# Five matmul groups and two DMA issues change places in a hand-written order

## The chip, the cores and the metric

The kernel runs on one core of a Trainium2 chip. The metric is the device time of one execution in microseconds (us); lower is better. A core has five engines that run their own instruction streams and meet through semaphores: TensorE (PE, matrix products into PSUM; its weight loads are shown apart as PEld), VectorE (DVE), ScalarE (ACT), GpSimd (POOL) and SyncE (SP, which here only issues DMAs). PSUM, where products land, has eight banks of 128 x 512 floats.

## What is computed

Two branches share one layer norm of q (2048 rows of 512), and their results are joined:

```python
xn = _layernorm(x)                                  # x = A_q
# branch A: a long convolution per channel, done in the reference with FFTs
k_shift = sum(k_pad[:, t:t + S, :] * shift_k[:, ks - 1 - t] for t in range(4))
kv = k_shift * v
y = causal_conv(kv, ssm_k) + kv * ssm_D             # over 2048 positions
s = xn * y
# branch B: a gated feed-forward layer, 512 -> 1792 -> 512
g = silu((gelu(xn @ w_gate) * (xn @ w_up)) @ w_down)
out = x + s * g
```

(The convolution and the sum over taps are abridged here.)

## The kernel before

**Branch A** is a Fourier transform in two stages, done as matrix products. Stage 1 multiplies by a table `F1`: for the filter (called H and J; its transposed halves are `HTr` and `HTD`) in `half1` (line 919) and `stage1_h` (line 929), for kv in `stage1_k` (line 956). kv is made in place in `V`, so the profile shows these last products as `psall<-V,F`; they are called V's products here, and there are two of them, each of two 512-column matmuls, for every index u from 0 to 7. A stage 1 product goes to a PSUM bank pair, is copied by ACT or DVE into a staging buffer (`AST`, `ASX`, or parts of `X` and `G` that are not in use yet), and is stored by DMA to `ZH` (filter) or `ZK` (kv) in device memory. Stage 2 loads blocks `BH` and `BK` from there in another order, multiplies in 32 x 32 tiles (line 1028), multiplies the two spectra and goes back.

**Branch B** works in four blocks q of 512 rows: transposes of the normalized rows (`xn_transpose`, line 841), 14 units of a gate and an up product (`unit`, line 1109), and the down products of four row tiles (`down`, line 1143), which are cut into three pieces of 4, 5 and 5 matmuls. All ordinary matmuls go through the helper at line 618, so the profile shows them with that line.

**The order is written out by hand.** Every piece of work is a numbered task; the string `SEQ` lists all tasks, and `Sched.run` (line 345) walks it. Each engine executes its tasks in the order in which they stand in `SEQ`; between engines only data and buffers order the work. While it walks, a planner with estimated durations also picks buffers: a pool (`Pool_.find`, line 250) gives the free slot that has been free the longest by the planner's estimate. PSUM banks come from three pools over the same eight banks: `psF` (one bank, at most four in use), `psC` (a pair of banks) and `psX` (one bank, for transposes). A slot is given back where the last task that reads it stands in `SEQ`, so a task's place in the list also decides which bank it can get. Semaphore waits are derived from the buffers, so every order that the planner can fill with slots is correct.

Three details matter around the change:

- The staging buffers of J are `X[12:14]`, `X[14:16]` and two parts of `G`; those of kv are three (`AST` 0, `AST` 1, `ASX`). The load of the fourth row block of q, `X3` (task 48, line 772), overwrites `X[12:16]` and so waits until every store to `ZH` has landed (line 981).
- SP issues its DMAs strictly in order: one that waits holds up all behind it.
- V's product u=6, part 0 (task 255) is copied out by task 256 into `AST` 0, which held u=2 before; 256 therefore waits until the store of u=2 (task 239) has landed. Task 262, a later product of V, needs the bank pair that 256 empties.

Tasks that are named below:

| task | engine | work |
|---|---|---|
| 84, 85 | PE | transposes of row tiles 2 and 3 of block 0 (four small matmuls each) |
| 109, 110 | PE, ACT | filter product `HTr` u=5, second half (two 256-column matmuls); its copy to staging |
| 370, 378 | PE | up products of block 0, units 0 and 1, first halves (four 256-column matmuls each) |
| 434, 438, 448 | PE | pieces of down products of block 0: 434 has five matmuls, 438 and 448 four each |
| 242, 243, 244 | PE, ACT, SP | V's product u=3, part 1; its copy; the store of u=3 to `ZK` |
| 250, 251 | PE, ACT | V's product u=5, part 0; its copy to `ASX`, which held u=3 |
| 137, 138, 139 | PE, ACT, SP | filter product J5; its copy; its store to `ZH` |
| 122, 123, 124 | PE, ACT, SP | filter product J0; its copy; its store to `ZH`, the last one |
| 48, 239 | SP | load of X3; store of u=2 to `ZK` |
| 526, 491 | PE | gate product of block 1, unit 13; up product of block 1, unit 4 (four 512-column matmuls each) |
| 257, 262 | PE | V's products u=6 part 1 and u=7 part 1 |
| 640, 646, 647 | DVE | layer-norm statistics of two tiles of X3 and an aggregation |
| 451, 452 | ACT, DVE | the gate function on the down product of task 448, which empties its bank |

The profile's names: `psall` is PSUM, `Wu`, `Wg` and `Wd` are the up, gate and down weights, `HT` is the hidden layer.

Of the kernel before, what the change touches and what calls it, by code (L numbers as in the profile page):

```python
# [25 lines left out]
ORDER = "x02 h0 h1 x22 w0 w1 h2 h3 D0 w2 s0 k0 v0 x1 w3 k1 v1 d0 d1 k2 v2 k3 v3 x2 x3"  # L26
SEQ = (
    "17 18 0 3 1 2 4 8 5 7 11 20 6 9 50 12 65 66 67 73 19 68 75 74 49 10 76 13 52 21 82 22 86 117 83 69 107 70 71 112 54 72 87 77 78 53 369 51 "
    "108 36 56b 79 84 371 109 88 80 370 15 85 372 23 31 89 110 378 377 113 27 373 379 381 383 375 14 453 455 457 380 24 458 374 459 25 454 118 "
    "382 119 55 456 460 32 120 376 389 102 384 397 399 28 30 33 461 34 29 37 63 38 111 385 387 393 16 59 463 386 103 462 388 464 391 398 104 26 "  # L30
    "400 390 395 105 465 146 394 405 396 99 147 121 466 148 468 150 407 57 409 100 401 403 46 392 402 406 149 151 470 35 404 152 39 96 413 408 "
    "469 410 472 153 467 411 101 415 473 412 421 154 414 416 58 471 155 422 417 61 423 424 106 429 156 97 114 158 93 60 62 431 44 425 426 427 428 "
    "115 418 498 159 43 419 98 420 41 94 90 160 502 500 91 499 95 474 475 92 501 476 161 157 518 504 503 430 81 477 225 432 478 520 227 479 116 "
    "162 226 480 505 163 40 228 506 134 519 166 164 521 42 167 481 140 183 45 508 229 135 168 514 141 143 136 144 515 128 486 516 517 129 230 488 "
    "490 169 232 507 47 231 131 165 170 492 125 142 443 233 433 126 132 509 171 482 240 444 445 137 184 241 234 235 174 172 127 138 64 236 175 "
    "434 242 133 145 438 446 243 173 122 439 182 123 245 484 176 177 246 440 130 178 247 435 447 179 248 180 139 237 238 181 250 244 448 441 436 "
    "437 124 249 48 483 449 252 251 450 253 485 260 239 451 261 640 255 646 647 452 510 512 185 442 511 256 513 257 642 491 258 262 526 644 643 "
    "190 263 487 254 186 493 641 527 645 259 264 195 648 489 528 187 522 494 188 189 495 529 649 496 523 652 524 651 191 192 650 716 540 525 535 "
    "497 550 556 552 196 536 557 553 193 197 265 537 198 538 266 554 267 270b 278 268 555 291 541 542 279 280 530 200 531 653 269 194 532 304 283 "
    "551 558 271 199 272 292 533 562 561 543 296 559 560 545 546 547 293b 534 544 273 539 682 654 274 276b 684 655 275 656 277 281 201 548 282 "  # L40
    "563 674 657 202 284 285 683 685 203 658 660 205 662 675 549 294 664 286 676 295 289 287 297 298 663 204 659 661 317 670 299 677 592 302 600 "
    "594 300b 301 305 665 306b 593 330 672 307 309 602 671 673 206 308 207 595 712 208 210 568 612 614 570 209 613 310 596 318 319 601 615 322b "
# [1244 lines left out]
```

## Time and profile before

| what | value |
|---|---|
| time, median of 3 runs | 196.22 us (195.83 to 196.37) |
| the profiled execution's own time | 195.05 us |
| its span, first to last instruction | 193.3 us |
| PE busy | 186.7 us, 97% |
| DVE, ACT busy | 159.8 us (83%), 125.0 us (65%) |
| DMA | 49.19 MB, mean 255 GB/s |

The profile is one execution. Its own time is 1.75 us above its span, for what lies around the instructions, and 1.17 us below the median of the runs. A matmul's record lasts longer than the engine needs before the next one can start, since matmuls are pipelined: rows of one kind show one start every 0.216 us for 512 columns, so time that PE loses is read between starts, and the "idle before" in brackets understates it. A few matmul records are missing (30 of the 32 of `psall<-V,F` are there).

### The profile page before, as it was taken

The page shows a single profiled execution, that of the slowest core. Times are in us where ns is not written, and L with a number is a line of the kernel's source. Part 1 is how long each engine was busy: PE and PEld are TensorE (multiplying, and loading weights), DVE is VectorE, ACT ScalarE, POOL GpSimd, SP SyncE. Part 2 cuts the span into 40 slices and gives each one's busy share as a digit, 9 for nine tenths or more (in the row PEclk, how much of TensorE's full clock was granted, in tenths as well). Part 3 has the DMA queues.
Part 4 walks back from the last instruction along what each step waited for, and adds up shares of the span by engine and source line. Part 5 has one row for each costly group of instructions (what it writes and reads, how often), then busy time and mean ns, then how long its engine had stood idle before and what let it go on. Part 6 is the DMA issues. An engine that isn't in the chain of part 4 may idle for free.

```text
span 193.3 us, 3491 instructions
## 1 busy us (share of the span) xinstructions
PE 186.7 (97%) x1364; PEld 84.7 (44%) x1377; DVE 159.8 (83%) x245; ACT 125.0 (65%) x170; POOL 13.9 (7%) x32
## 2 busy tenths in 40 slices
PE   7799999999999999999999999999999999999993
PEld 2674544444444344343434433433444334444442
DVE  6799879998999993977888789878897863588993
ACT  6788899969866987868548766856577431232121
POOL 5512600000000000020300000000000000000000
DMA  5999999899999868999999981892705344939433
GB/s 181 326 300 360 380 405 331 182 254 378 335 381 337 243 221 262 356 333 317 256 308 221 345 270 58 292 333 86 262 13 196 105 140 136 407 114 325 158 139 136
DMA packets 45958, 49.19 MB, mean 255 GB/s; under 512 B 12787, under 2 KB 39671, under 8 KB 45942
## 3 DMA queue, kind: packets, MB, share of 16 engines
q1 hardware_dynamic: 37366, 42.67, 69.5%
q10 hardware_dynamic: 8576, 6.29, 10.3%
q8 instruction: 11, 0.18, 0.4%
q14 instruction: 5, 0.04, 0.1%
HBM read 27.39 MB, written 14.68 MB: 218 GB/s over the span
## 4 chain that ended last, share of the span: by engine, by line
PE 80%; DMA 10%; ACT 3%; DVE 2%; issue 1%; POOL 1%; SPq 0%; ACTq 0%
PE psall L618 74%; DMA ZH<-X 5%; PE psall L1028 5%; DMA ZK<-AST 3%; DMA X<-in_A_q_dram 2%; ACT X L609 2%; POOL mv L832 1%; ACT AST L609 1%; DVE stats L821 1%; PE psall L854 1%; DVE XN L835 0%; ACT G L1164 0%; POOL mv L831 0%; DVE HTr L612 0%; DVE G L1175 0%
## 5 line engine op out<-in xcount | busy, mean ns | idle before, releaser
L618 PE MATMUL psall<-xnT,Wu 128*128 128x512 bf16 (+1 forms) x232 | 55.8, 372 | 0.0
L618 PE MATMUL psall<-xnT,Wg 128*128 128x512 bf16 (+1 forms) x232 | 55.3, 372 | 0.0
L618 PE MATMUL psall<-Wd,HT 128*128 128x512 bf16 (+2 forms) x231 | 50.8, 366 | 0.7 <-issue 0.5
L1140 DVE TENSOR_TENSOR HT<-psall,GE 128x512 bf16<-128x512 f32 x54 | 36.6, 685 | 15.3 <-PE psall L618 14.1
L1137 ACT ACTIVATE GE<-psall 128x512 bf16<-128x512 f32 x54 | 31.6, 600 | 13.7 <-PE psall L618 13.0
L618 PEld LDWEIGHTS psall<-Wd,HT 128*128 128x128 bf16 x238 | 22.4, 98 | 25.8 <-issue 1.1
L618 PEld LDWEIGHTS psall<-xnT,Wg 128*128 128x128 bf16 x232 | 22.0, 98 | 25.2 <-issue 1.3
L618 PEld LDWEIGHTS psall<-xnT,Wu 128*128 128x128 bf16 x232 | 21.6, 98 | 25.9 <-issue 3.5
L609 ACT ACTIVATE X<-psall 128x1024 bf16<-128x1024 f32 (+1 forms) x18 | 15.0, 842 | 3.9 <-DMA ZH<-X 3.7
L609 ACT ACTIVATE HS<-psall 128x1024 bf16<-128x1024 f32 x14 | 13.7, 1022 | 4.1 <-PE psall L1028 4.1
L1164 ACT ACTIVATE G<-psall 128x512 bf16<-128x512 f32 x12 | 7.0, 597 | 12.6 <-PE psall L618 12.4
L1011 DVE TENSOR_TENSOR KAC<-KAC,KTM 128x2048 bf16<-128x2048 bf16 x12 | 14.6, 1217 | 0.1
L1009 DVE TENSOR_TENSOR KTM<-KK,SKB 128x2048 bf16<-128x2048 bf16 x12 | 14.6, 1217 | 0.0
L609 ACT ACTIVATE BO<-psall 128x1024 bf16<-128x1024 f32 x9 | 9.1, 1023 | 8.2 <-PE psall L1028 7.7
L821 DVE BATCH_NORM_STATS2 stats<-X 128x6 f32<-128x512 bf16 x16 | 10.3, 676 | 3.8 <-DMA X<-in_A_q_dram 3.8
L609 ACT ACTIVATE KB<-psall 128x1024 bf16<-128x1024 f32 x11 | 11.0, 1021 | 3.6 <-PE psall L1028 3.6
L609 ACT ACTIVATE AST<-psall 128x1024 bf16<-128x1024 f32 x12 | 12.3, 1034 | 1.5 <-PE psall L618 0.9
L612 DVE CAST BO<-psall 128x1024 bf16<-128x1024 f32 x7 | 8.5, 1223 | 3.7 <-PE psall L1028 3.7
L1172 ACT ACTIVATE G<-psall 128x512 bf16<-128x512 f32 (+2 forms) x5 | 2.6, 512 | 13.1 <-PE psall L618 13.1
L1091 DVE TENSOR_TENSOR HW<-KB,HW 128x1024 bf16<-128x1024 bf16 x16 | 10.9, 682 | 0.0
L1091 DVE TENSOR_TENSOR HS<-KB,HS 128x1024 bf16<-128x1024 bf16 x16 | 10.8, 682 | 0.0
L618 PE MATMUL psall<-V,F 128*128 128x512 bf16 x30 | 8.8, 380 | 0.5 <-ACT AST L609 0.3
(83 smaller groups left out, 171.2 us busy)
## 6 DMA issues: line engine op xcount, KB each, us to landing
BH<-ZH SPq DMA_DIRECT2D x8, 512.0 KB, 5.8
HW<-HS SPq DMA_DIRECT2D x16, 256.0 KB, 3.3
BK<-ZK SPq DMA_DIRECT2D x8, 512.0 KB, 5.2
ZI<-BO ACTq DMA_DIRECT2D x16, 256.0 KB, 3.0
BI<-ZI SPq DMA_DIRECT2D x8, 512.0 KB, 4.5
ZK<-AST SPq DMA_DIRECT2D x6, 512.0 KB, 4.5
Hn<-in_A_ssm_k_dram SPq DMA_DIRECT2D x4, 512.0 KB, 8.0
KK<-in_A_k_dram SPq DMA_DIRECT2D x4, 512.0 KB, 8.9
```

The source lines that it names most:

```text
L609: return h.activation(o, i, ACTF.Copy, scale=scale)
L612: return h.tensor_copy(o, i)
L618: return h.matmul(o, lhsT=l, rhs=r, start=st, stop=sp)
L821: t_stats[t] = op([("DVE", 670.0)], lambda e, h, t=t: h.bn_stats(stats[:, t, :], X[:, t, :]), r=[bX[q][t % 4]], w=[bst[t]], rr=[R_X[t]], w ...
L1009: op([("DVE", dur)], lambda e, h, j=j, m=m: h.tensor_tensor(KTM[:, m.slot, :, :], kk(j), sk(j), ALU.mult), r=need + [bSKB[j], a], w=[m], r ...
L1011: op([("DVE", dur)], lambda e, h, m=m: h.tensor_tensor(KAC[:, a.slot, :, :], KAC[:, a.slot, :, :], KTM[:, m.slot, :, :], ALU.add), r=[m], ...
L1028: trk.op("PE", lambda h: h.matmul(ps(s, i)[b, :], lhsT=wt(col)[a, :], rhs=data(col)[a, :], start=n < 16, stop=n >= len(todo) - 16, tile_po ...
L1091: return hd.tensor_tensor(o, flat(KB, kb[h]), o, ALU.mult)
L1137: op([("ACT", act(512))], lambda e, h: h.activation(GE[:, g.slot, :], bank(pg), ACTF.Gelu_apprx_tanh), r=[pg], w=[g], rr=lambda: R_bank(pg ...
L1140: op([("DVE", dve(512, 1))], lambda e, h: h.tensor_tensor(HT[:, q % 2, m, :], bank(pu), GE[:, g.slot, :], ALU.mult), r=[pu, g], w=[bHT[q][m]],
L1164: op([("ACT", act(n))], lambda e, h, g=g, pc=pc: h.activation(g, pc(), ACTF.Tanh, scale=0.5), r=[p], w=[bt], rr=lambda p=p: R_bank(p), ww= ...
L1172: op([("ACT", act(n))], lambda e, h, g=g, pc=pc: h.activation(g, pc(), ACTF.Silu), r=[p], w=[bt], rr=lambda p=p: R_bank(p), ww=rg, after=z ...
```

## The change

Only the string `SEQ` differs:

```diff
-    "108 36 56b 79 84 371 109 88 80 370 15 85 372 ...
+    "108 36 56b 79 84 371 88 80 370 15 85 109 372 ...
...
-    "434 242 133 145 438 446 243 ... 246 440 130 178 247 435 447 179 248 180 139 237 238 181 250 244 448 441 436 "
-    "437 124 249 48 483 449 252 251 450 253 485 260 239 451 261 640 255 646 647 452 510 512 185 442 511 256 513 257 642 491 258 262 526 644 643 "
+    "434 438 242 133 145 446 243 ... 246 440 130 178 244 247 435 447 179 248 180 139 237 238 181 448 441 250 436 "
+    "437 124 249 483 449 252 251 450 253 485 260 451 261 48 640 239 255 452 510 646 512 185 442 511 256 513 257 642 258 647 526 262 644 643 491 "
...
-    "497 550 556 552 196 536 557 553 193 197 265 ...
+    "497 550 556 552 557 553 193 196 197 536 265 ...
```

Sorted by engine, this is what moves against work of the same engine:

| engine | before | after |
|---|---|---|
| PE | 84, 109, 370, 85, 378 | 84, 370, 85, 109, 378 |
| PE | 434, 242, 438, 122 | 434, 438, 242, 122 |
| PE | 237, 250, 448, 483 | 237, 448, 250, 483 |
| PE | 257, 491, 262, 526, 487 | 257, 526, 262, 491, 487 |
| DVE | 640, 646, 647, 452, 442, 513, 642, 644 | 640, 452, 646, 442, 513, 642, 647, 644 |
| SP | 130, 139, 244, 124, 249, 48, 239 | 130, 244, 139, 124, 249, 48, 239 |

The order on ACT, on POOL and in the list of loads stays as it is. The other moved numbers (48, 239, 451, 510, 512, 196, 536 and so on) pass only tasks of other engines; they change where slots are taken and given back. Nothing is added or removed: the same instructions run.

6 rows, old and new, of the table SEQ are left out of this document.

## The prediction

> **What bounds the kernel now.** I read the page first, then the waits of PE, then its timeline around each wait, then the chain, and last the DMA queue behind the wait that matters most.
>
> ```profile
> span 193.3 us, 3491 instructions
> PE 186.7 (97%) x1364; PEld 84.7 (44%) x1377; DVE 159.8 (83%) x245; ACT 125.0 (65%) x170; POOL 13.9 (7%) x32
> ```
>
> PE is busy from end to end. An edit can only win time in which PE waits, and a new wait costs its full length. Two of PE's waits, in the view of waits (a third stands in the timeline below):
>
> ```profile
> PE psall L618 <- ACT AST L609: 0.3, 1, 0.3
> PE psall L618 <- ACT X L609: 0.2, 1, 0.2
> ```
>
> PE's timeline around all three (start, length, work, in brackets the idle time):
>
> ```profile
> 9.94 0.40 PE L854 MATMUL psall<-ident,XN 128*128 128x128 bf16 x4
> 10.54 0.39 PE L618 MATMUL psall<-HTr,F 128*128 128x256 bf16 x2 [0.20 <-DVE HTr L612]
> 10.77 0.60 PE L618 MATMUL psall<-xnT,Wu 128*128 128x256 bf16 x4
> 11.21 0.39 PE L854 MATMUL psall<-ident,XN 128*128 128x128 bf16 x4
> 11.43 0.60 PE L618 MATMUL psall<-xnT,Wu 128*128 128x256 bf16 x4
> ...
> 59.05 0.61 PE L618 MATMUL psall<-V,F 128*128 128x512 bf16 x2
> 59.49 2.32 PE L618 MATMUL psall<-Wd,HT 128*128 128x512 bf16 x10
> 61.65 0.59 PE L618 MATMUL psall<-HTD,F 128*128 128x512 bf16 x2
> ...
> 62.51 1.24 PE L618 MATMUL psall<-Wd,HT 128*128 128x512 bf16 x5
> 63.92 0.60 PE L618 MATMUL psall<-V,F 128*128 128x512 bf16 x2 [0.17 <-ACT X L609]
> ...
> 77.96 1.03 PE L618 MATMUL psall<-xnT,Wu 128*128 128x512 bf16 x4
> 79.28 0.38 PE L618 MATMUL psall<-V,F 128*128 128x512 bf16 x1 [0.28 <-ACT AST L609]
> ```
>
> Ten matmuls from 59.49 to 61.65 give one start every 0.216 us; the four transposes from 11.21 give 0.055 each, the four short matmuls from 10.77 give 0.11. The time lost between starts is then: before 109, 10.54 - (9.94 + 0.22) = 0.38; before 242, 63.92 - (62.51 + 5 x 0.216) = 0.33. At 262 the record of the first of two matmuls is missing, so it began at 79.28 - 0.216 = 79.06; PE was free at 77.96 + 4 x 0.216 = 78.82. Lost: 0.24.
>
> The chain from 45 to 85 us says what the late ones hang on:
>
> ```profile
> 51.20 6.68 DMA ZH<-X
> ...
> 57.96 1.03 ACT X L609
> ...
> 59.01 3.81 DMA ZH<-X
> ...
> 62.84 1.03 ACT X L609
> ...
> 72.03 5.91 DMA ZK<-AST
> ...
> 77.97 1.03 ACT AST L609
> ```
>
> Each is a copy by ACT that waits until a store has left its staging buffer: a store to ZH for the product at 59.05 and for 242 (released at 62.84 + 1.03 = 63.87), and for 262 the store of u=2, task 239, landed at 72.03 + 5.91 = 77.94.
>
> **The change, part by part.**
>
> *109 behind 370 and 85.* DVE's timeline at this place:
>
> ```profile
> 9.80 0.68 DVE L612 COPY HTr<-psall 128x1024 bf16<-128x1024 bf16 x1
> 10.40 0.41 DVE L835 TENSOR_SCALAR XN<-X,mv 128x512 bf16<-128x512 bf16 x1
> ```
>
> DVE's copy ends at 10.48 and 109 started at 10.54, so a hop costs 0.06. In the new order 370 starts at 10.16 and ends at 10.60. 85 needs the rows that DVE ends at 10.81 and now waits itself, to 10.87; it ends at 11.09, 109 at 11.31. 378 started at 11.43, so PE is 0.12 ahead: a third of the wait, the rest has moved to 85. The three tasks exchange banks; following the planner's pick by hand, bank pairs are only renamed afterwards, and I find no new owner that would wait. PE does not keep the 0.12: at 59.05 it meets a copy whose store was 6.68 us in a full queue, and nothing here makes that queue shorter. I count 0; the ends are -0.12 and 0.
>
> *438 ahead of 242.* Four down matmuls fill the wait from 63.59, and 242 starts at 63.59 + 0.864 = 64.45, after its release. The 0.33 is gone. Behind it stands ACT:
>
> ```profile
> 63.76 1.02 ACT L609 ACTIVATE AST<-psall 128x1024 bf16<-128x1024 f32 x1
> 65.15 1.04 ACT L609 ACTIVATE ASX<-psall 128x1024 bf16<-128x1024 f32 x1
> 66.05 1.05 ACT L609 ACTIVATE X<-psall 128x1024 bf16<-128x1024 f32 x1
> ```
>
> Copy 243 (65.15) gets its product at 64.45 + 0.60 (the length of the pair at 63.92) = 65.05, still before ACT is free: covered by 0.1. 122, next on PE at 64.88, needs the pair that the first row empties at 64.78, with the hop 64.84: covered by 0.04; without that cover 122 is late by as much. PE runs 0.33 ahead from here to 262.
>
> *448 ahead of 250.* PE is dense here, so nothing is won. The copy of 250 stands on ACT behind two gate functions, which hide the 0.86 by which 250 comes later; without them its store would be late by up to 0.86, with nobody waiting before the second stage. 0.
>
> *526 in the place of 491, 452 earlier on DVE.* One group of four stands ahead of 262 before and after, so its wait gets no cover. But 526 needs the bank that 452 empties, and 452 stands behind 640, which waits for X3:
>
> ```profile
> 76.69 1.29 DVE L821 BATCH_NORM_STATS2 stats<-X 128x6 f32<-128x512 bf16 x2 [2.98 <-DMA X<-in_A_q_dram]
> 78.11 1.25 DVE L1166 SCALAR_TENSOR_TENSOR G<-G,psall 128x512 bf16<-128x512 bf16 x2
> ```
>
> Half of 1.29 each: 452 starts at 77.34, takes 0.63 to 0.7, and 526 can start near 78.05, ending at 78.91. PE would be there at 77.96 - 0.33 = 77.63. So most of the wait moves from 262 to 526; it ends ahead of the release of 262 at 79.06 with 0.15 to spare, and if X3 is later, both are later together. 491 and 647, which come later, have readers on DVE that are further behind. 0; beyond the cover it would cost what is over 0.15.
>
> *244 ahead of 139 on SP.* SP's timeline and its longest wait for a DMA, then the DMA queues from 66 to 74 us, first the rate in 40 slices of 0.2 us, and from the page the row of instruction fetches:
>
> ```profile
> 63.89 0.50 SPq L590 DMA_DIRECT2D ZH<-X  x1
> 66.21 0.33 SPq L590 DMA_DIRECT2D ZK<-ASX  x1
> 67.13 0.36 SPq L590 DMA_DIRECT2D ZH<-X  x1
> 71.64 0.34 SPq L590 DMA_DIRECT2D X<-in_A_q_dram  x1
> 72.03 0.43 SPq L590 DMA_DIRECT2D ZK<-AST  x1
> ```
>
> ```profile
> SPq L590 <- DMA ZH<-X: 1.3, 1, 1.3
> ```
>
> ```profile
> GB/s 277 67 0 0 0 307 451 451 389 287 328 341 236 274 292 282 172 23 20 20 41 20 15 164 392 389 392 471 389 389 82 20 0 143 184 184 205 164 164 61
> q8 instruction: 1, 0.02, 1.1%
> ZK<-ASX SPq DMA_DIRECT2D x1, 512.0 KB, 4.7
> ZH<-X SPq DMA_DIRECT2D x1, 256.0 KB, 4.5
> ```
>
> ```profile
> q8 instruction: 11, 0.18, 0.4%
> ```
>
> 139, issued at 63.89 so far, now stands behind 244, which waits for copy 243 until 66.21; so 139 goes out at 66.54, between the store of u=3 and 124 (67.13), the last store to ZH. X3 waits for 124 to land (67.13 + 4.5 = 71.6; it is issued at 71.64), and 239 stands behind X3 on SP. So whatever delays the landing of 124 delays X3, then 239, then the copy that releases 262.
>
> Does 139's 256 KB delay it? From 67.0 to 69.4 the queue moves at about 320 GB/s; then, for six slices, at some 20 GB/s, about a sixteenth: one of the 16 DMA engines is behind and the others are idle. An instruction fetch falls into this window. (The fetches are PE's, I infer: 2741 instructions over 11 fetches are 249 for each.) That engine carries a sixteenth of every transfer, and 139 now adds 16 KB to it, at 20 GB/s 0.8 us, ahead of 124's share. On the other side the fetch follows PE's progress, and PE is 0.33 ahead: the engine is free that much sooner. I take 0.8 - 0.33, about 0.45, and keep 0.8 (the fetch stays) as the upper end. At the lower end the fetch misses these stores; then no engine is behind, three stores of 512, 256 and 256 KB are through 3.2 us after 67.0, at 70.2, before the tail ends today (70.6 at least), and 124 lands up to 1 us sooner.
>
> The Trainium skill (DMA: Bandwidth & Descriptors, section Why a DMA increments its semaphore by 16 and not by 1) says that a DMA has landed only when each of its engines has posted its share. The trace agrees: fifteen sixteenths of the traffic are through at 69.4, and the store counts as landed at 71.6.
>
> *The rest* (196 behind 193, 48, 239 and others in the list) passes no task of its own engine. 0.
>
> **The sum.** PE reaches 262 at 78.82 - 0.33 = 78.49, with or without profit: 262 starts when 256 is done, at 79.06 + 0.45 = 79.51. From there on PE has no wait worth naming, and DMA and PE move together. The profiled execution's 195.05 would become 195.5; the median, 1.17 above it, 196.22 + 0.45, rounded to 196.65. The 0.33 is real where it is made and is lost 15 us later.
>
> **The rivals.**
>
> - *Slower by 0.4%:* the lagging engine does not get its fetch any sooner. 124 lands 0.8 later and so does 262: 197.0. It decides once the delay of 239 exceeds 0.59. For it: the 20 GB/s tail is there, 139 is put ahead of 124. Against: the fetch moves with PE.
> - *Faster by 0.3%:* the fetch does not coincide with these three stores, or is short. 124 then lands by 71.0 or sooner, X3 and 452 move with it, 256 is released before PE arrives, and both the 0.33 and the 0.24 are won: 195.65, with the 0.12 of the first place 195.5. It decides once 239 lands 0.57 earlier. Against: the store of u=3 is issued at 66.21 in both orders and the fetch moves by only a third of a us. The Trainium skill (Runtime: NRT & Kernel Launch, section Instruction fetch mechanics) says that a sequencer refills by its own DMA queue while it executes, and that the cost is mostly hidden. By that rule this rival would be the likeliest; the slices at 20 GB/s beside a fetch speak against it.
> - *Nothing moves:* the longer share and the earlier fetch cancel, 262 stays at 79.06: 196.2.
>
> **How the numbers follow.** I give the forecast (a shift of 0.2 to 0.59) 0.32, no movement (-0.5 to 0.2) 0.22, the slower rival 0.28, the faster one 0.18. What counts as no change is within 0.3%, 0.59 us, about what a measurement of this kernel can tell. The slower rival lies beyond; the faster one sits at the bound, and I count most of it as faster. So faster 0.16, same 0.56, slower 0.28. The range is from 195.6 to 197.1: the ends are the faster rival and the slower one with 0.1 for 122 and 526.
>
> **What would show it.** Right: no wait left at the product at 63.9; SP's DMA of X3 issued after 72.0; a new wait of 0.7 to 0.9 before a gate product near 78.5, released by DVE, and a short one at V's product behind it; a tail at some 20 GB/s in the DMA queue near 70 that is longer than now. Wrong: X3 issued before 71.6, or any PE wait between 80 and 190 us, where there is none now. If PE's row at 59 begins earlier than 59.0, the first edit's 0.12 lives on, against what I say.

## The result and the profile after

| | before | after |
|---|---|---|
| time, median of 22 runs each, same chip | 195.64 us (194.51 to 197.21) | 196.23 us (195.16 to 197.25) |
| ratio after / before, 95% interval | | 1.0041 [1.0023, 1.0060] |
| the profiled execution's own time | 195.05 us | 195.16 us |
| its span | 193.3 us | 193.4 us |
| granted clock of PE | 1.000 | 0.999 |

The changed kernel is slower by 0.41%, or 0.8 us (0.45 to 1.2). The medians of the table lie closer together, 0.59 us or 0.30%, so the size is only roughly known. Forecast were +0.45 us and a time of 196.65 us, in a range from 195.6 to 197.1. The time lies in the range and the shift is above the forecast. By the prediction's bound of 0.3% the case is "slower" and not "the same", though the interval begins below that bound. The base has moved as well: the kernel before has a median of 195.64 us here, where the forecast started from 196.22. On this base the forecast would be 196.09, its range 195.0 to 196.5, and 196.23 lies in that too.

The page's first lines of the kernel after look like those of before:

```profile
span 193.4 us, 3490 instructions
PE 186.9 (97%) x1364; PEld 84.8 (44%) x1377; DVE 159.6 (83%) x245; ACT 125.4 (65%) x170; POOL 13.9 (7%) x32
```

In the view of PE's waits, the 0.2 us for the copy into `X` (V's product 242) is gone, and the wait for the copy into `AST` (product 262) has grown from 0.3 to 1.1:

```profile
PE psall L618 <- ACT AST L609: 1.1, 1, 1.1
```

PE's timeline after, at the places that the prediction showed of before (start, length, work, in brackets the idle time):

```profile
9.62 0.39 PE L854 MATMUL psall<-ident,XN 128*128 128x128 bf16 x4
9.96 0.60 PE L618 MATMUL psall<-xnT,Wu 128*128 128x256 bf16 x4
10.49 0.40 PE L854 MATMUL psall<-ident,XN 128*128 128x128 bf16 x4
10.72 0.38 PE L618 MATMUL psall<-HTr,F 128*128 128x256 bf16 x2
10.94 0.60 PE L618 MATMUL psall<-xnT,Wu 128*128 128x256 bf16 x4
...
58.68 0.59 PE L618 MATMUL psall<-V,F 128*128 128x512 bf16 x2
...
62.13 2.11 PE L618 MATMUL psall<-Wd,HT 128*128 128x512 bf16 x9
64.07 0.59 PE L618 MATMUL psall<-V,F 128*128 128x512 bf16 x2
64.50 0.59 PE L618 MATMUL psall<-HTD,F 128*128 128x512 bf16 x2
...
77.24 1.03 PE L618 MATMUL psall<-xnT,Wg 128*128 128x512 bf16 x4
79.39 0.38 PE L618 MATMUL psall<-V,F 128*128 128x512 bf16 x1 [1.13 <-ACT AST L609]
79.61 1.89 PE L618 MATMUL psall<-xnT,Wu 128*128 128x512 bf16 x8
81.43 0.43 PE L1028 MATMUL psall<-BH,TF 32*32 32x512 bf16 x16
```

To set beside them, two rows of the kernel before that the prediction did not show:

```profile
65.23 0.59 PE L618 MATMUL psall<-HTD,F 128*128 128x512 bf16 x2
...
81.31 0.43 PE L1028 MATMUL psall<-BH,TF 32*32 32x512 bf16 x16
```

Absolute times mislead here. This execution reached V's product near 59 us 0.37 us earlier than that of before (58.68 against 59.05), for reasons that have nothing to do with the stretch that follows. So everything below is measured from that product. From it to the first product on `BH` (L1028) took 81.31 - 59.05 = 22.26 us before and 81.43 - 58.68 = 22.75 after: 0.49 more. From there to the end of the span both need the same, 111.94 and 111.93 us, with the same order of work. The whole difference inside the spans is made in this one stretch. (The tables below are worked out with three decimals and show 22.27 and 0.48.)

Within the stretch the rows show a gain and a loss. Task 122, behind 242, starts 64.50 - 58.68 = 5.82 after the reference product, not 65.23 - 59.05 = 6.18: PE is 0.36 ahead. Then 526 ends its starts at 77.24 + 4 x 0.216 = 78.10, and 262 (its first record is missing, as before) begins at 79.39 - 0.216 = 79.17: 1.07 lost, where the kernel before lost 0.24.

SP's timeline and, below it, the chain after, show why:

```profile
65.75 0.33 SPq L590 DMA_DIRECT2D ZK<-ASX  x1
66.13 1.38 SPq L590 DMA_DIRECT2D ZH<-X  x2
...
71.79 0.35 SPq L590 DMA_DIRECT2D X<-in_A_q_dram  x1
72.18 0.43 SPq L590 DMA_DIRECT2D ZK<-AST  x1
```

```profile
72.18 5.89 DMA ZK<-AST
...
78.09 1.03 ACT AST L609
```

The row with x2 holds 139 (66.13) and 124 (66.67). By 124's record it lands 5.10 us after its issue (4.49 before), X3 goes out when it has landed, 239 behind X3, and 262 behind the copy that waits for 239. All of them, counted from the reference product, are 0.5 later: X3's issue 13.11 (12.59 before), the landing of 239 19.39 (18.89).

The DMA queues from 66 to 74 us, rate in slices of 0.2 us, then the instruction fetch and the stores to ZH:

```profile
GB/s 0 0 82 389 430 369 307 328 471 238 328 266 292 271 266 289 271 292 254 31 330 471 392 410 348 474 185 41 20 20 41 20 20 41 82 123 102 246 287 184
q8 instruction: 1, 0.02, 0.8%
ZH<-X SPq DMA_DIRECT2D x2, 256.0 KB, 5.0
```

The slices at some 20 GB/s, in which by the prediction's reading one engine works and the others wait, were at 69.4 to 70.6 before. Now they stand from 71.4 to 72.6, most of them after 124 has landed (66.67 + 5.10 = 71.77), behind the store that 249 issued in the meantime. The fetch is shorter: 0.8% of 16 engines over 8 us are 1.0 us, before 1.1% or 1.4. Its record starts at 68.06 (67.41 before), which is 9.38 after the reference product where it was 8.36: later, not earlier.

### The profile page after: what moved, and what is told of

Its sections match the earlier page's. It is cut to its first block, busy times and chain, and to the rows that moved or that the text cites. A ratio compares the mean times of both kernels' runs of the same rounds, so it can differ in the third digit from the quotient of the medians.

```text
span 193.4 us, 3490 instructions
## 1 busy us (share of the span) xinstructions
PE 186.9 (97%) x1364; PEld 84.8 (44%) x1377; DVE 159.6 (83%) x245; ACT 125.4 (65%) x170; POOL 13.9 (7%) x32
## 4 chain that ended last, share of the span: by engine, by line
PE 91%; DMA 3%; ACT 3%; issue 1%; DVE 1%
PE psall L618 84%; PE psall L1028 5%; DMA ZK<-AST 3%; ACT AST L609 1%; PE psall L854 1%; PE psall L878 1%; ACT G L1164 1%; ACT HTr L609 1%; DVE G L1175 0%; DVE G L1174 0%; ACT ASX L609 0%; ACT G L1172 0%; DVE AST L671 0%
## 5 line engine op out<-in xcount | busy, mean ns | idle before, releaser
L618 PEld LDWEIGHTS psall<-Wd,HT 128*128 128x128 bf16 x238 | 22.4, 98 | 25.9 <-issue 1.1
```

Source lines behind the costliest of these rows:

```text
L618: return h.matmul(o, lhsT=l, rhs=r, start=st, stop=sp)
```

## The experiments

Two theories. *The queue*: the swap on SP puts 139's share on the lagging engine ahead of 124, everything behind 124 is late, and PE's 0.36 is given back with interest at 262. *The order of PE and the banks*: 526 ahead of 262, with new owners of banks, makes the wait. All kernels compute the whole reference. Each kernel below has one profiled execution and, from e1 on, 12 timed runs beside 35 of the kernel before:

| kernel | V's product near 59 | first BH product | stretch between | BH to end | 124, issue to landing | third fetch, length | ratio to before, 95% |
|---|---|---|---|---|---|---|---|
| before | 59.05 | 81.31 | 22.27 | 111.94 | 4.49 | 1.46 | 1 |
| after | 58.68 | 81.43 | 22.75 | 111.93 | 5.10 | 1.00 | 1.0041 [1.0023, 1.0060] |
| e1_sp_back | 59.30 | 81.89 | 22.59 | 111.95 | 4.74 | 1.59 | 1.0005 [0.9976, 1.0033] |
| e2_sp_only | 59.16 | 81.93 | 22.77 | 111.97 | 5.12 | 0.92 | 1.0017 [0.9993, 1.0042] |
| e3_fetch | 58.90 | 82.07 | 23.17 | 111.94 | 5.58 | 1.67 | 1.0015 [0.9984, 1.0045] |
| e4_store_first | 58.93 | 80.86 | 21.93 | 111.94 | 4.29 | 0.94 | 0.9992 [0.9969, 1.0015] |
| e5_down_only | 60.28 | 82.24 | 21.96 | 112.25 | 4.24 | 1.17 | 1.0019 [0.9993, 1.0044] |
| e6_fetch44 | 59.16 | 82.24 | 23.08 | 111.95 | 3.56 | 1.16, elsewhere | 1.0004 [0.9981, 1.0028] |
| e7_g_first | 59.47 | 81.15 | 21.68 | 112.23 | 4.25 | 0.89 | 0.9962 [0.9936, 0.9989] |
| e8_store_only | 59.63 | 81.65 | 22.02 | 111.97 | 4.42 | 0.92 | 1.0012 [0.9986, 1.0038] |
| e9_bk_first | 59.85 | 81.54 | 21.69 | 111.94 | 4.25 | 0.88 | 0.9999 [0.9976, 1.0023] |
| e10_swap_store_first | 58.68 | 80.90 | 22.22 | 111.94 | 4.66 | 1.14 | 1.0006 [0.9983, 1.0030] |
| e11_first_only | 58.94 | 81.07 | 22.13 | 112.19 | 4.60 | 1.65 | 1.0014 [0.9989, 1.0038] |
| e12_changed_again | 59.17 | 81.99 | 22.82 | 111.94 | 5.07 | 0.93 | 1.0045 [1.0023, 1.0067] |

Most intervals of the ratios reach 0.25% to both sides, 0.5 us, as much as the stretch changes. Where an execution comes to V's product near 59 us differs too, from 58.68 to 60.28 (in e5 the product waited 1.20 us, in the kernel after not at all), and the timed runs of one kernel scatter by more than that. So the mechanism is read from the stretch, which begins behind this scatter, and the ratio confirms only the large differences.

**SP back to the old order** (on the kernel after).

```diff
-130 178 244 247 ... 248 180 139 237
+130 178 139 247 ... 248 180 244 237
```

> The changed kernel with one thing undone: on SP the store of J5 (139) goes out before the store of u=3 (244) again, as in the kernel before; every PSUM bank is the changed kernel's. Theory A (the swap on SP delays the last store to ZH, with it X3 and the store of u=2): 124 lands about 0.8 us earlier against the copies on ACT, V's product 262 waits some 0.7 to 0.8 less than the 1.13 of the changed kernel, and the time is 195.4, ratio to before 0.997 to 1.000. Rival B (the loss comes from the matmul and DVE order or from the exchanged banks, the DMA queue is only noise): 196.2, ratio 1.003 to 1.005, the wait of 262 stays near 1.1.

The stretch was 22.59: 0.16 less than after, not back at 22.27 less PE's gain. 124 landed in 4.74 us, not 5.10, but this execution's fetch was long, 1.59. That is less than the 0.7 to 0.8 expected: 262 still waits 0.90 between starts with SP's old order, so the swap is not the only thing that sets 124's landing. The ratio, 1.0005, lies nearer to the first theory than to the second, but its interval reaches into both.

**The swap alone** (on the kernel before).

```diff
-248 180 139 237 ... 181 250 244 448
+248 180 244 237 ... 181 250 139 448
```

> The kernel before with only the swap on SP: 244 ahead of 139; every PSUM bank and the order on all other engines as before. Theory A: 124 lands 0.8 us later, since PE is not ahead here and the instruction fetch does not move; V's product 262 waits 0.24 + 0.8, ratio to before 1.004 (1.003 to 1.005), 196.4. Rival B: 1.000, within 0.0015, the wait of 262 stays at 0.28.

The stretch grew by 0.50, as much as by the whole change. The chain of this kernel is the one that the queue theory draws:

```profile
67.10 5.12 DMA ZH<-X
...
72.24 0.34 SPq L590
...
72.63 5.93 DMA ZK<-AST
...
78.59 1.03 ACT AST L609
```

PE's order here is that of before, so neither 526 nor anything else on PE is needed for the loss at 262. Of the ratio, 1.003 to 1.005 was expected and 1.0017 measured, with an interval that holds 1 as well as the 1.0041 of the whole change: the timed runs alone do not show that the swap costs anything.

**The fetch moved.** PE's warm-up, matmuls on a zero tile before the real work, was cut into more and shorter ones, so that the instruction count at which PE fetches falls earlier in the work (both on the kernel after; 11 matmuls of 512 columns before).

```diff
-N_WARM = 11          # 512 columns each
+N_WARM = 22          # e3: 256 columns each
+N_WARM = 44          # e6: 128 columns each
```

> The changed kernel with its 11 warm-up matmuls of 512 columns made 22 of 256 columns: the same columns on PE before the first real work, but 22 more PE instructions (a load and a matmul each), so every later instruction fetch comes some 11 matmuls, 2.4 us, earlier in PE's work; banks and all orders as in the changed kernel. Theory A with the fetch as the cause of the lagging DMA engine: the fetch falls near 64.7 us instead of 67, is over before the store of u=3 moves, the stretch at 20 GB/s is gone, 124 lands over 1 us earlier (near 70.5 on the trace's clock), the wait of 262 is at most 0.3, the time 195.0 to 195.2, ratio to before 0.995 to 0.998. If another thing makes that engine lag: nothing changes, ratio 1.003 to 1.005 and the slow stretch stays.

> The changed kernel with 44 warm-up matmuls of 128 columns in place of 11 of 512: the same columns, 66 PE instructions more, so that the third instruction fetch comes some 7 us earlier in PE's work than the 68.06 of the changed kernel. Theory A2 (the fetch that falls on one DMA engine beside the store of u=3 makes the tail): with the fetch before 66 us, the stretch at some 20 GB/s after the store of J0 is gone, that store (124) lands 3.5 to 4 us after its issue in place of 5.1, 262 has a wait of 0.3 at most, the stretch from V's product at 59 to BH is 21.9, ratio 0.996 to 0.999. Rival E (that engine lags for another reason): the tail stays, 124 takes 5 us, the stretch 22.7, ratio 1.002 to 1.005.

The fetches are PE's, as the prediction inferred: the second one starts at 39.97 in the kernel after, at 35.66 in e3 and at 32.48 in e6, where only PE's warm-up differs. The third followed the count less well. In e3 it started at 67.32, only 0.74 us earlier for 11 more matmuls with their weight loads, and took 1.67 us. It stayed among the three stores and 124 needed 5.58 us; from the DMA queues, 66 to 74 us:

```profile
q8 instruction: 1, 0.02, 1.3%
ZH<-X SPq DMA_DIRECT2D x2, 256.0 KB, 5.5
```

That is the swap with a long fetch: a stretch of 23.17, 0.90 over before, which in the trace is the rival "slower by 0.4%". The ratio, 1.0015, does not show it. In e6 the fetch started at 59.94 and left the stores near 68 alone: 244 landed in 2.68 us (4.63 after), 124 in 3.56, and 262 did not wait. But it met other stores to ZH: one issued at 61.06 took 3.99 us, where the same store takes 2.56 in the kernel after. Its window of the DMA queue from 59 to 67 us, the first line, and PE's waits that follow, the other two:

```profile
q8 instruction: 1, 0.02, 0.9%
```

```profile
65.46 0.61 PE L618 MATMUL psall<-V,F 128*128 128x512 bf16 x2 [0.73 <-ACT X L609]
66.38 0.61 PE L618 MATMUL psall<-HTD,F 128*128 128x512 bf16 x2 [0.31 <-ACT AST L609]
```

So the fetch does slow the stores that it meets, by about 2 us on a store of 512 KB. Moving it moved the harm, and the stretch came to 23.08, not the 21.9 expected.

**239 ahead of X3.** If the chain 124, X3, 239 makes the wait, then a store issued before X3 must end it, whatever the swap does. e4 does this with SP's old order otherwise (e1 plus this edit), e8 on the kernel before, e10 on the kernel after with its swap.

```diff
-451 261 48 640 239 255     (e4, e10)
+451 261 239 48 640 255
-249 48 483 ... 260 239 451 (e8)
+249 483 ... 260 239 48 451
```

> The changed kernel with two orders on SP altered: 139 before 244 again, and the store of u=2 (239) ahead of the load of X3 (48). Some later PSUM banks (after 86 us) differ. Theory A: 239 no longer waits for the last store to ZH nor stands behind 512 KB of X3; it goes out near 71.0 and lands by 75, 262 has no wait, PE keeps all it wins: 195.0 to 195.2, ratio 0.995 to 0.998; the wait, if any, moves to what needs X3 or the BH load near 81 us. Rival B: 196.2, ratio 1.003. Rival C (the DMA queue is full up to 85 us, so the time reappears at the stage 2 product near 81 us): no wait at 262, but one of 0.5 or more before the product of BH, ratio 0.999 to 1.002.

> The kernel before with one move on SP: the load of X3 (48) behind the store of u=2 (239); PE, ACT and DVE as before, banks as before up to 81 us. Theory A2: 239 goes out near 71.4 and lands near 74.5, so the wait of 262 (0.24 between starts) goes; the stretch from V's product at 59 to BH 22.0 to 22.1, ratio 0.998 to 1.000. Rival F (PE's waits there are set by ACT's queue, not by the store): 262 still waits, 22.27.

> The changed kernel with one move on SP: the store of u=2 (239) ahead of the load of X3 (48); the swap of 244 and 139 stays. Theory A2 (the swap costs only through the last store to ZH, X3 behind it, and 239 behind X3): the last store to ZH still takes about 5 us to land, but 239 lands by 75, the wait of 262 goes, the stretch from V's product at 59 to BH is 21.9 to 22.1 in place of 22.75, ratio 0.997 to 1.001. X3 is late by the swap, so 0.3 to 0.6 can reappear before the up product that waits for 442. Rival B (the swap costs in another place): the stretch stays above 22.5.

In all three the wait at 262 is gone: 239 lands 3.1 us after its issue (e4 3.14, e8 3.14, e10 3.12), where the change needs 5.89 behind X3. e8 keeps before's wait at 242 and loses nothing later: 22.02, 0.25 below before, which is the 0.24 that the kernel before lost at 262. e4 has both gains, 0.57, and comes to 21.93, 0.34 below before: it loses 0.25 at 79.89 to a DVE instruction that frees a bank, and its ratio, 0.9992, is not the 0.995 to 0.998 expected. e10 comes to 22.22 (21.9 to 22.1 expected), since the swap delays X3 too, and with it DVE's statistics 640, behind which 452 and 442 stand. Its PE and DVE rows:

```profile
78.33 0.38 PE L618 MATMUL psall<-V,F 128*128 128x512 bf16 x1
78.74 1.04 PE L618 MATMUL psall<-xnT,Wu 128*128 128x512 bf16 x4
79.93 1.04 PE L618 MATMUL psall<-xnT,Wu 128*128 128x512 bf16 x4 [0.15 <-DVE G L1166]
```

```profile
77.41 0.69 DVE L821 BATCH_NORM_STATS2 stats<-X 128x6 f32<-128x512 bf16 x1 [4.40 <-DMA X<-in_A_q_dram]
78.02 0.67 DVE L1166 SCALAR_TENSOR_TENSOR G<-G,psall 128x512 bf16<-128x512 bf16 x1
```

The up products start 0.41 and 1.19 us after what stands before them, where 0.216 and 0.864 are needed: 0.20 and 0.32 lost, both waiting for a bank that a DVE instruction behind the statistics empties. This is the wait that the prediction had put at 526; it exists, behind 262, and shows once 262 no longer hides it.

**452 and 442 ahead of 640** (on e4).

```diff
-451 261 239 48 640 255 452 510 646 512 185 442 511
+451 261 239 48 255 452 442 640 510 646 512 185 511
```

> The kernel with the store of u=2 ahead of the load of X3 (stretch 21.93, one wait of 0.25 of an up product for 442, a DVE task that stands behind 640, which waits for X3), now with 452 and 442 ahead of 640 on DVE. The wait of 0.25 goes and nothing takes its place: stretch 21.6 to 21.7, ratio to before 0.996 to 0.999. Rival: the product of BH waits for its load (landed 80.2 there, 0.6 before it was needed): then the stretch stays at 21.9.

The stretch is 21.68, 0.59 below before: both gains, and no wait left in it. At 91 us there is a new one, for a load of `BK`, and with it the time from BH to the end grows by 0.29:

```profile
81.15 0.43 PE L1028 MATMUL psall<-BH,TF 32*32 32x512 bf16 x16
...
91.05 0.44 PE L1028 MATMUL psall<-BK,TF 32*32 32x512 bf16 x16 [0.21 <-DMA BK<-ZK]
```

This is the one kernel that is clearly faster than before: ratio 0.9962 [0.9936, 0.9989], 0.7 us.

**The load of BK ahead of one of HW's swaps** (on e7), to take that last wait away.

```diff
-494 188 189 495 ... 197 536 265 537
+494 188 265 189 495 ... 197 536 537
```

> The fastest kernel so far (0.9962 of before: J5's store first, the store of u=2 ahead of X3, 452 and 442 ahead of 640) with one more move on SP: the first load of BK (265) ahead of the two swap transfers of the first filter block (189); all banks as there. There the first product of BK waited 0.29 for that load. Theory A2 (what PE wins ahead of 79 us is taken back wherever it next meets the DMA queue): the 0.29 goes, the time from BH's first product to the end returns from 112.23 to 111.94 us, ratio to before 0.994 to 0.997. Rival G (the load lands no sooner, since it waits for the last store of ZK in either order): 112.2, ratio 0.996.

The trace did what was expected (21.69, and 111.94 to the end), the time did not: 0.9999 [0.9976, 1.0023]. The profiled execution lost 0.88 us at 59 us and 0.53 near 25 us; whether the earlier load does this, or chance, was not settled. The intervals of e7 and e9 overlap, so e7's gain in time rests on its own comparison alone.

**The down products alone** (438 ahead of 242 and the move of 196, on the kernel before), and **the first edit alone** (109).

```diff
-434 242 133 145 438 446 ... 552 196 536 557 553 193 197 265   (e5)
+434 438 242 133 145 446 ... 552 557 553 193 196 197 536 265
-84 371 109 88 80 370 15 85 372                                (e11)
+84 371 88 80 370 15 85 109 372
```

> The kernel before with one matmul edit alone: 438 ahead of 242 (and 196 behind 193 in the list, without which the planner finds no bank pair; banks before 86 us are as before). Between the start of V's product near 59 us and the first product of BH, the kernel before takes 22.27 us and the changed one 22.75. Theory A2 (PE's 0.33 is given back at 262, which is released by the DMA queue, and the instruction fetch only adds some tenths either way): no wait at the product near 63.9, a wait of about 0.6 at 262, the stretch 22.1 to 22.6, ratio 0.998 to 1.002. Rival D (the 0.33 is a gain that the SP swap alone destroys): the stretch 21.9 or less, ratio 0.998 or less.

> The kernel before with the first edit alone: 109 behind 370 and 85. My account: PE is 0.12 ahead after 85 and 109 and loses it before V's product near 59 us, which waits for a copy held by a store; the stretch from that product to BH 22.2 to 22.4, ratio 0.999 to 1.001. Rival: the 0.12 lives on to the end, ratio 0.9994, which this measurement cannot tell; the trace can, by the wait at 59.

e5 wins 0.31 in the stretch, about what the wait at 242 cost, and 262 waits 0.27 between starts, hardly more than before's 0.24. That is less than the 0.6 expected, because the release came earlier too: this execution's fetch was shorter than before's (1.17), 124 landed in 4.24, and the store of u=2 landed 18.59 after the reference product, not 18.89. It loses 0.31 again at one place:

```profile
89.22 0.75 PE L1028 MATMUL psall<-BH,TF 32*32 32x512 bf16 x16
89.90 2.33 PE L618 MATMUL psall<-Wd,HT 128*128 128x512 bf16 x10
```

Sixteen matmuls on BH take 0.37 (81.80 - 81.43 in PE's timeline after), so the down products start 0.31 late. By the list of banks they get one that 193 fills and empties last; that this is the reason was argued, not tested, and the whole change has no such loss. e11 is 0.14 shorter in the stretch (22.13, where 22.2 to 22.4 was expected) and 0.25 longer behind it, at the load of BK again (90.93). Its ratio, 1.0014, tells neither from nothing.

**The change once more.**

> The changed kernel as it is, profiled a second time and timed beside the three others. If the place and the length of the third instruction fetch (68.06, 1.00 us) belong to the program, the stretch from V's product at 59 to BH comes out at 22.7 to 22.8 again and the last store to ZH takes 5.1 us; if they differ from execution to execution, it can lie anywhere from 22.5 to 23.2. Ratio 1.002 to 1.005.

Ratio 1.0045 [1.0023, 1.0067], stretch 22.82, 124 in 5.07 us, fetch 0.93 us long. Both the loss and its place are those of the first comparison.

Put together, the column of 124's landing sorts roughly by two causes:

- *The swap.* With a fetch of 0.9 to 1.2 us, 124 lands in 4.24 to 4.42 us without the swap, in the mean 4.29 (e4, e5, e7, e8, e9), and in 5.07 to 5.12 with it, in the mean 5.10 (after, e2, e12): 0.81. With a fetch of 1.6 to 1.7 us it is 4.60 and 4.74 without (e11, e1) and 5.58 with the swap (e3): 0.91.
- *The length of the fetch.* One that is longer by 0.66 (1.62 against 0.96 in the mean) costs 4.67 - 4.29 = 0.38, one longer by 0.72 with the swap 0.48: 0.6 to 0.7 us for each.

e10 (swap, 1.14, 4.66) does not fit, and it can't be set aside: up to the load of X3 it issues the same work in the same order as the kernel after. Against e5, whose fetch has nearly its length and place, the swap costs only 0.42 there. So the swap costs 0.4 to 0.9 us, by the execution.

The length goes with the place: fetches that start 0.2 to 0.4 us after 124's issue last 1.14 to 1.67 us (before, e1, e3, e5, e10, e11), those that start 1.3 to 1.8 after it 0.88 to 1.00 (after, e2, e4, e7, e8, e9, e12). Which is cause and which effect was not separated. Nor does the change set the place. From the reference product the fetch starts after 8.36 us in before, but after 9.55 in e2 and 9.64 in e8, which have PE's order of before; and after 9.38 in the kernel after and 9.55 in its repetition, but after 8.18 in e10. Outside e6 it falls in one of two places, 8.2 to 8.4 or 9.3 to 9.8 us after that product, and what chooses between them stays open.

## Why the prediction came out as it did

*109 behind 370 and 85: the 0 holds, its working is not shown.* From the transposes 84 to 378 PE needs 10.94 - 9.62 = 1.32 us, not 1.49: 0.17 won, 0.12 forecast. What is left of the wait stands ahead of 370 (9.96, due at 9.62 + 0.22 = 9.84) and of 85 (10.49, due at 9.96 + 0.44 = 10.40). But the wait ahead of 109 belongs to one execution: without this edit the same pieces need 1.10 us in e2 and e8 and 1.17 in e5, with it 1.16 to 1.33 in all the others. So no run shows that the edit wins anything. Nor is the 0.12 given back at 59, as the prediction had it. From 378 to the product near 59 the kernel after needs 47.73 us, before 47.61; about as much is lost at an up product near 24.7, the product at 59 itself does not wait in the kernel after, and e11 needs 47.55. That the row at 59 begins before 59.0, named as a sign against this, came from an earlier start of the execution.

*438 ahead of 242: right, with its cover.* The wait at 63.92 is gone and PE 0.36 ahead (0.33 forecast). 122 is not late, so the cover of 0.04 held. The gain is lost at 262, as forecast; in e4 and e7, where 262 does not wait, it stays.

*448 ahead of 250, and the rest: right* at 0. From BH to the end the kernels before and after agree within 0.01 us.

*526 in the place of 491: wrong.* The step that failed is "526 needs the bank that 452 empties". By the order in which banks are given back it takes one that 510 used and 512 empties; the trace does not name banks, but it shows that 526 did not wait for 452. It starts at 77.24, 0.20 ahead of the DVE instruction (77.44) that it was to wait for:

```profile
76.83 0.70 DVE L821 BATCH_NORM_STATS2 stats<-X 128x6 f32<-128x512 bf16 x1 [3.76 <-DMA X<-in_A_q_dram]
77.44 0.67 DVE L1166 SCALAR_TENSOR_TENSOR G<-G,psall 128x512 bf16<-128x512 bf16 x1
```

So no wait of 0.7 to 0.9 stands before the gate product; the whole 1.07 is at 262. On the sum this cost nothing, since 262 was the later of the two in any case. A bank's owner followed by hand through a few hundred tasks is a weak step, and it should have been priced as open.

*The swap on SP: the path right, one of its two terms wrong, and the sum close by luck.* The path from 139 over 124, X3 and 239 to 262 is what the traces show. The first term, 16 KB on a lagging engine at 20 GB/s for 0.8 us, was measured at 0.81 and 0.91, but at 0.42 in e10. Its size does not show its cause: 256 KB more in a queue that moves the prediction's 320 GB/s would be 0.8 us as well, and no run separates the two, for which one without the swap and without a fetch beside it would be needed. The second term, "the fetch follows PE's progress, and PE is 0.33 ahead", failed. The fetch started 1.0 us later against the reference product, not 0.33 earlier, and in e3 22 more instructions ahead of it moved it by 0.74 us only. What took its place is the fetch's length: 1.00 instead of 1.46 us, at 0.6 to 0.7 worth 0.28 to 0.32. So it came later and was shorter, and e2 and e8, with PE's order of before, show that this is not the change's doing. The two terms leave 0.5 of 124's time from issue to landing, measured were 0.61; less 0.09 for an earlier issue of 124 that makes the 0.5 that arrives at 262. The sum of +0.45 stands beside +0.48 in the trace of the change and +0.55 in its repetition, but its second term was right by size and wrong by cause. In an execution with a fetch like that of e3 the same swap costs 0.90: the rival at 0.8.

The Trainium skill (Runtime: NRT & Kernel Launch, section Instruction fetch mechanics) says that the cost of crossing a 16 KiB boundary of the instructions is mostly hidden. For the stores beside the fetch that does not hold here: 244's store needs 2.68 us in e6 without the fetch beside it, 4.63 in the kernel after with it. What the fetch costs PE itself was not measured.

*The signs.* X3 is issued at 71.79, not after 72.0, yet 0.52 later against the reference product: absolute marks were the wrong kind of sign. The tail is hardly longer, six to seven slices in place of six, and stands at 71.4, not near 70. There is no new wait of PE between 80 and 190 us.

*The size and the chances.* The ratios say 0.8 and 0.9 us (0.45 to 1.2 and 0.45 to 1.3), the traces 0.48 and 0.55. The two fit at the lower end of the intervals, and fetches of e3's length in some executions would make up the rest, but no run shows how the length is spread: that stays open. The other kernels with the swap do not clearly repeat the loss in time, with ratios of 1.0017 (e2), 1.0015 (e3) and 1.0006 (e10, where 239 goes first). "Within 0.3%" had the largest chance, because the 0.33 was taken off: the 0.8 had slices of the queue behind it, the 0.33 only an inference on which engine fetches and when. The rival with 0.8 deserved more than 0.28.

## What to carry to other kernels

Where a queue is strictly in order, follow a swapped DMA to everything behind it: here a store moved by one place delayed another store, a load behind that, a store behind the load, and at last PE, and with the store issued ahead of the waiting load PE's wait was gone. Put a gain at the place where it is made and then look for the next wait behind it that a fixed event ends; until that event moves, the gain is only carried to it. Compare traces from a common piece of work, not from the start, and write the signs of a prediction in such differences.

## What the runs showed of the hardware

- One instruction fetch of PE, 16 KB in one packet (0.18 MB in 11), took 0.9 to 1.7 us, and stores that met it landed late: 512 KB in 4.63 us (after) against 2.68 (e6). The length of the third fetch varied by 0.8 us between kernels and went with its place among the stores; for one kernel profiled twice it was 1.00 and 0.93.
- The start of the third fetch did not move in proportion to the number of instructions ahead of it: 22 more moved it by 0.74 us (e3), 66 more by 8.1 (e6). With the same order on PE it fell 8.36 or 9.64 us after the same product (before, e8), so one execution does not tell where it falls.
- A store of 512 KB behind the load of X3 landed 5.9 us after its issue (after: 5.89), ahead of it 3.1 to 3.6 (e4 3.14, e9 3.63), at the same place in the same queue.
